# Attention and spectral mixing on one core: complex mode weights read in 16 KB rows, two modes on the two halves of the partitions

## The chip, the cores and the metric

The kernel runs on one core of a Trainium2 chip. The metric is the device time of one execution, in microseconds (us), as the median of three runs. The inputs and the output are float32. A trace of one execution, taken by the hardware profiler, goes with the times.

## The reference, cut to what matters

Two stages follow each other. The first is attention over a sliding window of 128 keys with a distance bias, on q, k, v of shape (8 batches, 8 heads, 576 tokens, 64). Its result is laid out as x of shape (8, 576, 512). The second stage mixes x in the frequency domain:

```python
X = np.fft.rfft(x, axis=1)                       # x: (8, 576, 512)
Xr, Xi = real(X[:, :64]), imag(X[:, :64])        # the 64 lowest modes
Yr = einsum('bmd,mde->bme', Xr, w_r) - einsum('bmd,mde->bme', Xi, w_i)
Yi = einsum('bmd,mde->bme', Xr, w_i) + einsum('bmd,mde->bme', Xi, w_r)
y = np.fft.irfft(Yr + 1j * Yi, n=576, axis=1)    # other modes are zero
u = x + y
out = u + np.maximum(u @ w_ch, 0.0)              # (8, 576, 512) float32
```

`w_r` and `w_i` are (64 modes, 512, 512) float32, 67 MB each. Every mode has its own complex matrix, and each is used once, for the 8 batches.

## The kernel before

**Attention.** The work is cut into 16 units: a batch and four of its heads. The list `STAGE` writes out by hand the order in which the steps of neighbouring units are issued: cast, transpose, evacuate, score, exp, mask, value, norm. Loads of q, k and v go out on SyncE's queue, two units ahead, each as soon as the raw tile that it fills has been cast. After a batch's second unit `spectrum` multiplies the batch's x by the table `F` of cosines and sines (TensorE, 20 matmuls, weights x of 128 channels taken every fourth, moving 128 columns of `F`), and `channels` copies the result from PSUM into `XC` (mostly on ScalarE), the stationary operand of the weight products. The spectrum's PSUM tile shares its buffer (`tp`) with the transposes of q and k.

**Weights.** A unit of weights is one matrix of one mode, 1 MB in HBM, cast to bfloat16 by the DMA that GpSimd issues: 128 partitions, each with four neighbouring rows of the matrix (8 KB read, 4 KB written). There are 127, since the imaginary matrix of mode 0 multiplies zeros. `load_w` loads single units: 14 into the pool `early`, 7 into the raw tiles that attention has finished with (`spare`), and 8 again into `early` (`again`). In attention a tiny copy by GpSimd (`gate`, L565) holds each load back until a cast of k is done. `load_packs` loads two units with one DMA (L491) into 6 and later 8 buffers, or one by one (L499) for the last four modes. The last unit comes in three parts.

**Products.** For a unit, four matmuls (L886) contract over 128 partitions each: `XC` gives 32 stationary columns (16 for the real, 16 for the imaginary output, 8 batches each), the weights are the 512 moving columns, and the result goes to 32 rows of the PSUM tile `acc`. The units of two modes go side by side on two column groups of the array. Four modes make a quad. `quad_end` scales it into bfloat16 (L608), transposes it (L612) and copies it to `YT`. From the ninth quad on, a list `side` gives TensorE one piece of other work at each step: `stream_spectra` (L631 to L637), `project` (L702, L711) and `augment` (L726 to L734), that is the inverse transform and the channel product of the first 32 modes. `warm` (L688) issues matmuls without use.

**The end.** For the last quad `late_end` and the code after the loop scale the late rows, transpose them, and patch the rows of the last modes into `Z` and `ZW` by small DMAs (`patch`, L648). Then 18 pieces of output are finished: a relu on ScalarE (L802), a sum on VectorE (L842), and a store on SyncE's queue.

Of the kernel before, what the change touches and what calls it, by code (L numbers as in the profile page):

```python
# [34 lines left out]
NC = 24  # L35

# [70 lines left out]
class _Attention:  # L107


    def __init__(self, tc, ctx, q, k, v, consts, x, XC, raw):  # L110
        self.tc, self.nc = tc, tc.nc
        self.q, self.k, self.v = q, k, v
        self.ident, self.F, self.FT = consts
# [256 lines left out]
    def spectrum(self, u, _):  # L370
        nc = self.nc
        b, g = self.units[u]
        if g < self.NG - 1:
            return
        NM = self.F.shape[2] // 2

        last = u == len(self.units) - 1
        xt = self.ps.tile([P, 2, 4, 2, NM], FP32, tag="tp")
        for a in range(4):
            for st in range(FULL + 1):  # L380
                nc.tensor.matmul(
                    xt[:, a // 2 if last else 0, a].rearrange("p r m -> p (r m)"),
                    lhsT=self.x[:, b, st, a::4],
                    rhs=self.F[:, st + (b % 2 if st == FULL else 0)].rearrange(
                        "p (m r) -> p r m", r=2),
                    start=(st == 0), stop=(st == FULL),
                )
        self.open["xt", u] = xt

    def channels(self, u, _):  # L390

        nc = self.nc
        b, g = self.units[u]
        if g < self.NG - 1:
            return
        xt = self.open.pop(("xt", u))
        NM = self.F.shape[2] // 2
        view = self.XC[:, : 4 * NC * NM].rearrange(
            "p (q s t b m) -> p q t s b m", q=2, s=3, t=2, b=8)[:, :, :, :, b]
        if u < len(self.units) - 1:  # L400
            src = xt[:, 0].rearrange("p (q t) r m -> p q t r m", q=2)
            nc.scalar.copy(view[:, :, :, 1:], src)
            nc.scalar.mul(view[:, :, :, 0], src[:, :, :, 1], -1.0)
        else:
            lo, hi = slice(0, 2), slice(2, 4)
            nc.scalar.copy(view[:, 0, :, 1:], xt[:, 0, lo])
            nc.scalar.mul(view[:, 0, :, 0], xt[:, 0, lo, 1, :], -1.0)
            nc.vector.tensor_copy(view[:, 1, :, 1:], xt[:, 1, hi])
            nc.vector.tensor_scalar_mul(view[:, 1, :, 0], xt[:, 1, hi, 1, :], -1.0)
# [3 lines left out]
def kernel(  # L413
# [21 lines left out]
    XC = const.tile([P, 4 * NC * NM + 16 * NM], BF16, name="XC")  # L435
    ident = const.tile([P, P], BF16, name="ident")
    F = const.tile([P, FULL + 2, 2 * NM], BF16, name="F")
    FT = const.tile([P, 2, S], BF16, name="FT")
    gate = const.tile([P, 8], BF16, name="gate")
# [14 lines left out]
    turns = []  # L454
    for g in range(NM // 4):
        for m in range(4 * g, 4 * g + 4, 2):
            turns += ([[2 * m, 2 * m + 2], [2 * m + 1, 2 * m + 3]] if g < LAST
                      else [[2 * m], [2 * m + 1], [2 * m + 2], [2 * m + 3]])
    spot = {i: k for k, i in enumerate(i for turn in turns for i in turn)}
    turns[1].remove(1)  # L460
    wq, homes, todo_w, again = {}, {}, [i for turn in turns for i in turn], []

    def load_w(n, pool, chosen=None):

        for i in ([i for i in todo_w if i not in again][:n] if chosen is None else chosen):
            todo_w.remove(i)
            src = (moe_w_r, moe_w_i)[i % 2][i // 2].rearrange("(p a) e -> p a e", a=4)
            homes[i] = pool
            t = spare.pop(0) if pool is None else pool.tile([P, 4, DM], BF16, tag="w", name="w")
            for part in ((slice(0, 4),) if i < 2 * NM - 1  # L470
                         else (slice(0, 2), slice(2, 3), slice(3, 4))):
                nc.gpsimd.dma_start(out=t[:, part], in_=src[:, part])
            wq[i] = [t[:, a] for a in range(4)]

    def load_packs(n, pool):

        for _ in range(n):
# [3 lines left out]
            assert len(pack) == 2  # L481
            t = pool.tile([P, 2, 4, DM], BF16, tag="w", name="w")
            kinds = {i % 2 for i in pack}
            for s, i in enumerate(pack):
                todo_w.remove(i)
                homes[i] = pool if s else False
                wq[i] = [t[:, s, a] for a in range(4)]
            m, w = pack[0] // 2, (moe_w_r, moe_w_i)
            if len(kinds) == 1:
                assert pack[1] == pack[0] + 2  # L490
                nc.gpsimd.dma_start(  # L491
                    out=t.rearrange("p s a e -> p s (a e)"),
                    in_=w[kinds.pop()][m : m + 2].rearrange("m (p a) e -> p m (a e)", a=4))
                continue
            for s, i in enumerate(pack):
                src = w[i % 2][i // 2].rearrange("(p a) e -> p a e", a=4)
                for part in ((slice(0, 4),) if i < 2 * NM - 1
                             else (slice(0, 2), slice(2, 3), slice(3, 4))):
                    nc.gpsimd.dma_start(out=t[:, s, part], in_=src[:, part])  # L499

    with ExitStack() as actx:
        at = _Attention(tc, actx, q, k, v, (ident, F, FT), x, XC, raw)
# [26 lines left out]
        nc.gpsimd.memset(XC[:, 4 * NC * NM :], 0.0)  # L529
# [40 lines left out]
    with ExitStack() as mctx:  # L570
# [13 lines left out]
        def late_end(acc):  # L584

            rows = slice(0, 96)
            yq = pool.tile([P, DM], BF16, tag="yq", bufs=3)
            nc.vector.tensor_scalar_mul(yq[rows], acc[rows], 2.0 / S)
            patch([(nc.gpsimd, b) for b in range(2, B)], yq, lambda b: Z[:, b // 2, 1], 0, 6)
            yield  # L590
            tr = lps.tile([P, 4, P], BF16, tag="tr", name="tr")
# [13 lines left out]
        def quad_end(acc, g):  # L605

            yq = pool.tile([P, DM], BF16, tag="yq", bufs=3)
            nc.vector.tensor_scalar_mul(yq, acc, 2.0 / S if g else norm)  # L608
# [4 lines left out]
            hf, mm = g // 8, 4 * (g % 8)  # L613
            for ri in range(2):
                src = tr.rearrange("p e (j c) -> p e c j", c=32)[:, :, 16 * ri : 16 * ri + B]
                dst = YT[:, hf, :, :, mm : mm + 4, ri]
# [240 lines left out]
        quads, side, recycle = [], [], list(again)  # L857
        ZW = Z = XW = FM = FC = pairs = wch = w2 = None
        K1 = spot[again[-1]]
        for g in range(NM // 4):  # L860
            if g == 0:
                lps.tile([P, 2, 4, P], BF16, tag="tr", name="tr")
            acc = (lps if g % 2 else ps).tile([P, DM], FP32, tag="acc", bufs=1, name="acc")
            if g == LAST:
                part_acc = ps.tile([P, DM], FP32, tag="pa", bufs=1, name="pa")
            for i in range(8):
# [13 lines left out]
                now = turns.pop(0) if turns and spot[turns[0][0]] == k else []  # L880
                for a in range(4):
                    for t in now:
                        m, ri = t // 2, t % 2
                        c0 = (a // 2 * 2 * NC + 16 * (1 - ri) + a % 2 * 8) * NM + m
                        into = part_acc if g == LAST and m < NM - 1 else acc
                        nc.tensor.matmul(  # L886
                            into[32 * (m % 4) : 32 * (m % 4) + 32],
                            lhsT=XC[:, c0 : c0 + 31 * NM + 1 : NM], rhs=wq[t][a],
                            start=(ri == 0 and a == 0), stop=(ri == (m > 0) and a == 3),
                            tile_position=(0, 32 * (m % 4)),  # L890
                        )
                own = next((t for t in homes if spot[t] == k), None)
                if own is None:
                    continue
                if recycle:
                    load_w(1, early, [recycle.pop(0)])
                elif homes[own] not in (early, None, False):
                    load_packs(1, homes[own])
# [33 lines left out]
                elif g > LAST - 2 and k < 2 * NM - 1 or g == LAST - 2 and not side:  # L932
                    warm()
                if g == LAST and i == 5:
                    quads.append(late_end(part_acc))
                    next(quads[0])
            if g < LAST:
                quads.append(quad_end(acc, g))
                next(quads[0])
# [5 lines left out]
            elif g == LAST - 1:  # L945
# [8 lines left out]
        zl = zps.tile([P, DM], FP32, tag="z0", name="zl")  # L954
        nc.tensor.matmul(zl, lhsT=ident, rhs=wch[:, 0], start=True, stop=True)
        sides = (slice(0, DM // 2), slice(DM // 2, DM))
        trs = (lps.tile([P, 4, P], BF16, tag="tr", name="tr"),
               zps.tile([P, 4, P], BF16, tag="z1", name="tr1"))
        for i, c in enumerate(sides):
            nc.scalar.mul(yq[96:, c], acc[96:, c], 2.0 / S)  # L960
            for et in (2 * i, 2 * i + 1):
                nc.tensor.transpose(trs[i][:, et, 96:], yq[96:, et * P : (et + 1) * P],
                                    ident[96:, 96:])
            nc.vector.tensor_copy(yT[:, 2 * i : 2 * i + 2, 96:],
                                  trs[i][:, 2 * i : 2 * i + 2, 96:])
        patch([(nc.sync, 0), (nc.gpsimd, 1)], yq, lambda b: Z[:, b // 2, 1])
        patch([(nc.gpsimd, b) for b in (2, 3, 4, 5, 6)], yq, lambda b: Z[:, b // 2, 1], 6)
# [4 lines left out]
        for i, c in enumerate(sides):  # L972
            zl = zps.tile([P, DM], FP32, tag=f"z{i}", name=f"zl{i}")
# [14 lines left out]
        patch([(nc.gpsimd, 7)], yq, lambda b: Z[:, b // 2, 1], 6)  # L988
# [40 lines left out]
```

## Time and profile before

| | |
|---|---|
| median of 3 runs | 437.81 us (437.63 to 439.78) |
| the profiled execution, its own time | 437.99 us |
| its span, first to last instruction | 436.1 us |
| TensorE, busy | 316.2 us (73%), 3488 matmuls |
| VectorE, busy | 184.5 us (42%) |
| ScalarE, busy | 162.3 us (37%) |
| GpSimd, busy | 90.2 us (21%) |
| read from HBM, written to it | 162.53 MB, 9.44 MB |
| mean granted TensorE clock | 0.862 |

Engines in the profile are PE (TensorE matmul), PEld (TensorE weight load), DVE (VectorE), ACT (ScalarE), POOL (GpSimd) and SP (SyncE); a "q" behind a name is the engine's queue of issues. L886 is line 886 of the kernel. GB/s in the profile counts the bytes written, so a weight that is read as float32 and written as bfloat16 counts half of what is read. The share of the DMA engines adds up the times of their packets, and packets of one DMA engine overlap a little, so it can be above 1. A matmul's own time in the profile includes its way through the array; how dense a run of them is shows in the distance from start to start.

### The profile page before, as it was taken

To read this page: it belongs to the slowest core of one execution; us is meant where nothing else is said; L and a number is where in the kernel's file an instruction comes from. 1 tells how busy PE (TensorE), PEld (TensorE's weight loads), DVE (VectorE), ACT (ScalarE), POOL (GpSimd) and SP (SyncE) were. 2 spreads that over 40 slices of the span, in tenths; PEclk is the share of its full clock that TensorE was granted. 3 is DMA by queue.
4 is the path that set the end of the run, shared out by engine and by line. 5 is a ranking of instruction groups with operands and counts; after the bars stand their busy time and mean duration, and the time that the engine had idled before them with its cause. 6 is when DMAs were issued, how large, how long until landed. Compare 5 with 4: busy or idle time off the path is not lost.

```text
span 436.1 us, 8292 instructions
## 1 busy us (share of the span) xinstructions
PE 316.2 (73%) x3488; PEld 177.7 (41%) x3509; DVE 184.5 (42%) x332; ACT 162.3 (37%) x211; POOL 90.2 (21%) x170
## 2 busy tenths in 40 slices
PE   5589899979686635543442487999889999788982
PEld 4367677757565312111111133444434444334430
DVE  7789799887783301000000021322213233122684
ACT  6949899988681000000000011322222322102780
POOL 8701010103424002222112110101111110012600
PEclk9969999999999955555555569999999999989997
DMA  8999999999999999999999999999999999998598
GB/s 285 326 311 310 290 316 300 307 298 299 252 217 212 215 215 213 214 214 214 215 212 214 214 215 214 215 214 215 215 214 214 215 215 215 213 215 153 190 378 311
DMA packets 50453, 105.54 MB, mean 242 GB/s; under 512 B 4032, under 2 KB 21072, under 8 KB 50416
## 3 DMA queue, kind: packets, MB, share of 16 engines
q0 software_dynamic: 19440, 68.41, 77.9%
q1 hardware_dynamic: 30976, 36.60, 25.3%
q8 instruction: 27, 0.44, 0.4%
q14 instruction: 10, 0.08, 0.1%
HBM read 162.53 MB, written 9.44 MB: 394 GB/s over the span
## 4 chain that ended last, share of the span: by engine, by line
DMA 71%; PE 10%; DVE 8%; issue 5%; POOL 2%; ACT 1%; SPq 1%; DVEq 0%; POOLq 0%; ACTq 0%
DMA w<-in_moe_w_i_dram 42%; DMA wch<-in_moe_w_ch_dram 8%; DMA qr<-in_q_dram 7%; DMA vr<-in_v_dram 6%; DVE o L842 3%; DMA qr<-in_moe_w_i_dram 3%; PE my L702 2%; DMA vr<-in_moe_w_r_dram 2%; DMA kr<-in_k_dram 2%; DVE vb L246 1%; PE acc L886 1%; PE av L344 1%; POOL Z L648 1%; PE my L659 1%; DVE att L318 1%
## 5 line engine op out<-in xcount | busy, mean ns | idle before, releaser
L886 PE MATMUL acc<-w,XC 128*32 128x512 bf16 x456 | 80.3, 478 | 68.5 <-DMA w<-in_moe_w_i_dram 34.2
L886 PEld LDWEIGHTS <-XC 128*32 128x32 bf16 x508 | 38.4, 147 | 109.2 <-issue 82.8
L307 ACT ACTIVATE att<-sc 128x1024 bf16<-128x1024 f32 x64 | 64.1, 1032 | 9.7 <-PE sc L297 9.6
L636 ACT CAST ZW<-zw 128x512 bf16<-128x512 f32 x8 | 4.7, 585 | 142.9 <-PE zw L634 142.9
L344 PE MATMUL av<-vb,att 128*128 128x132 bf16 (+1 forms) x576 | 38.4, 217 | 13.3 <-DVE x L360 8.6
L344 PEld LDWEIGHTS <-att 128*128 128x128 bf16 x704 | 36.6, 98 | 18.7 <-DVE x L360 12.0
L608 DVE TENSOR_SCALAR yq<-acc 128x512 bf16<-128x512 f32 x14 | 9.6, 687 | 81.8 <-PE acc L886 81.8
L702 PE MATMUL my<-wch,xT 128*64 128x512 bf16 x288 | 34.5, 381 | 5.7 <-ACT x L733 4.2
L711 ACT CAST XW<-my 128x512 bf16<-128x512 f32 x36 | 19.3, 589 | 50.5 <-PE my L659 50.5
L683 DVE COPY xT<-tr 128x1024 bf16<-128x1024 bf16 x18 | 12.4, 692 | 54.9 <-PE tr L681 54.9
L269 ACT COPY qkT<-tp 128x1152 bf16<-128x1152 bf16 x30 | 33.5, 1116 | 4.1 <-PE tp L263 3.6
L491 POOL DMA_DIRECT2D w<-in_moe_w_r_dram x22 | 15.6, 710 | 72.1 <-PE acc L886 46.1
L491 POOL DMA_DIRECT2D w<-in_moe_w_i_dram x23 | 16.3, 709 | 64.1 <-PE acc L886 45.3
L297 PE MATMUL sc<-qkT 64*64 64x256 bf16 (+2 forms) x640 | 25.1, 263 | 4.8 <-ACT qkT L269 1.2
L360 DVE TENSOR_TENSOR x<-av,rec 128x640 bf16<-128x640 f32 x32 | 26.4, 825 | 1.1
L702 PEld LDWEIGHTS <-xT 128*64 128x64 bf16 x288 | 17.1, 109 | 21.5 <-issue 9.1
L246 DVE CAST vb<-vr 64x1024 bf16<-64x1024 f32 x32 | 22.6, 708 | 0.2
L733 ACT CAST x<-my 128x512 bf16<-128x512 f32 x18 | 10.5, 585 | 31.6 <-PE my L659 31.6
L297 PEld LDWEIGHTS <-qkT 64*64 64x64 bf16 x640 | 14.5, 109 | 19.1 <-issue 16.0
L734 DVE CAST x<-my 128x512 bf16<-128x512 f32 x18 | 12.4, 692 | 21.7 <-PE my L659 21.7
L842 DVE TENSOR_TENSOR o<-yy,r 128x1024 f32<-128x1024 f32 (+1 forms) x20 | 20.3, 1059 | 2.1 <-ACT r L802 1.9
L318 DVE TENSOR_TENSOR att<-att,mask 128x1024 bf16<-128x1024 bf16 x32 | 20.5, 682 | 0.0
(137 smaller groups left out, 424.7 us busy)
## 6 DMA issues: line engine op xcount, KB each, us to landing
w<-in_moe_w_i_dram POOLq DMA_DIRECT2D x23, 1024.0 KB, 36.2
w<-in_moe_w_r_dram POOLq DMA_DIRECT2D x22, 1024.0 KB, 35.6
qr<-in_q_dram SPq DMA_DIRECT2D x16, 576.0 KB, 7.9
kr<-in_k_dram SPq DMA_DIRECT2D x16, 576.0 KB, 7.9
w<-in_moe_w_r_dram POOLq DMA_DIRECT2D x16, 512.0 KB, 14.2
vr<-in_v_dram SPq DMA_DIRECT2D x56, 128.0 KB, 7.6
w<-in_moe_w_i_dram POOLq DMA_DIRECT2D x13, 512.0 KB, 24.0
out_dram<-o SPq DMA_DIRECT2D x13, 512.0 KB, 5.0
```

The lines of the kernel that those rows point to most:

```text
L246: nc.vector.tensor_copy(self.vb[u % 2][row, :, :, :, W * half : W * half + D], src[row, :2])
L269: (self.nc.vector.tensor_copy if u < 2 and w == "q" else self.nc.scalar.copy)(dst.rearrange("q h (p j) -> q h p j", j=TPP), tp.rearrange(" ...
L297: nc.tensor.matmul(sc[64 * half : 64 * half + 64, e, j * 256 + c0 : j * 256 + c0 + n], lhsT=qkT[row, 1, h, k0 + j : k0 + P : 2], rhs=qkT[r ...
L307: self.nc.scalar.activation(self.att[u % 2][:, kt * 8 * P : (kt + 1) * 8 * P], sc.rearrange("p e n -> p (e n)"), AF.Exp, scale=1.0 / math. ...
L318: nc.vector.tensor_tensor(out=rows, in0=rows, in1=self.table[:, heads], op=ALU.mult)
L344: nc.tensor.matmul(bank[:, qt * W : qt * W + rhs[j].shape[1]], lhsT=att[:, o : o + P], rhs=rhs[j], start=(n == 0 and j == 0), stop=(n == l ...
L360: nc.vector.tensor_tensor(out=self.x[:, b, :, cs].rearrange("p t (h d) -> p h t d", h=2), in0=tiles[:, :, :, :D], in1=rec.unsqueeze(-1).br ...
L491: nc.gpsimd.dma_start(out=t.rearrange("p s a e -> p s (a e)"), in_=w[kinds.pop()][m : m + 2].rearrange("m (p a) e -> p m (a e)", a=4))
L702: nc.tensor.matmul(mm[ROWS[half]], lhsT=lhsT, rhs=wch[:, dt], start=(dt == 0), stop=False, skip_group_check=True,)
L711: nc.scalar.copy(XW[:, j, n], mms[n])
L842: nc.vector.tensor_tensor(out=o[:, c], in0=yy[:, c], in1=r[:, c], op=ALU.add)
L886: nc.tensor.matmul(into[32 * (m % 4) : 32 * (m % 4) + 32], lhsT=XC[:, c0 : c0 + 31 * NM + 1 : NM], rhs=wq[t][a], start=(ri == 0 and a == 0 ...
```

## The change

A pack is now one kind of matrix (real or imaginary) of two neighbouring modes: the even mode on partitions 0 to 63, the odd one on 64 to 127, eight neighbouring rows of a matrix to a partition. In HBM a pack is one stretch of 2 MB, and each partition's row is 16 KB read and 8 KB written. `load_packs` loads a pack with one DMA; only the last pack comes in four parts. `load_w` loads half a pack (four of the eight rows of each partition, 8 KB read). The order of packs is real, real, imaginary, imaginary for each two pairs of modes (`seq`).

The spectra follow that layout. A second table `F2` holds the modes sorted by even and odd (33 columns each for real and imaginary, `XM`), copied from `F` by GpSimd at the start. `spectrum` makes 80 matmuls for a batch in place of 20, with 64 stationary columns (every eighth channel), 66 moving ones, alternately on the two column halves of the array. `XC` has the even modes' channels on partitions 0 to 63 and the odd modes' on 64 to 127.

A product now contracts over 64 partitions, so a pack has 16 matmuls. Even modes go to one PSUM tile and odd ones to another, and two packs are interleaved so that four neighbouring matmuls sit on four different tiles of the array (two row halves, two column groups). Products are issued when four steps have gathered (two packs), or one pack in the last quad; buffers are given back then. Two PSUM tiles hold eight modes, and `quad_end` runs twice after every second quad. In the last quad modes 60 and 61 are finished early and 62 and 63 late (before: 60 to 62 early).

```diff
+XM = 33
...
-        for a in range(4):
+        xt = self.ps.tile([P, 8, P], FP32, tag="tp")
+        for a in range(8):
             for st in range(FULL + 1):
...
+                for par in range(2):
+                    nc.tensor.matmul(
+                        xt[64 * par : 64 * par + 64, a, : 2 * XM],
+                        lhsT=self.x[:, b, st, (a + 4 * par) % 8 :: 8],
+                        rhs=self.F2[:, st + (b % 2 if st == FULL else 0), par].rearrange(
+                            "p r m -> p (r m)"),
+                        start=(st == 0), stop=(st == FULL), tile_position=(0, 64 * par),
+                    )
...
+    def pack_rows(p):
+
+        w, m = (moe_w_r, moe_w_i)[p % 2], p // 2 * 2
+        return w[m : m + 2].rearrange("m (p a) e -> (m p) a e", a=8)
...
+            nc.gpsimd.dma_start(out=t, in_=rows[:, 4 * (i % 2) : 4 * (i % 2) + 4])
...
-                nc.gpsimd.dma_start(
-                    out=t.rearrange("p s a e -> p s (a e)"),
-                    in_=w[kinds.pop()][m : m + 2].rearrange("m (p a) e -> p m (a e)", a=4))
...
+            for part in ((slice(0, 8),) if p < PACKS - 1
+                         else (slice(0, 4), slice(4, 6), slice(6, 7), slice(7, 8))):
+                nc.gpsimd.dma_start(out=t[:, part].rearrange("p a e -> p (a e)"),
+                                    in_=rows[:, part].rearrange("p a e -> p (a e)"))
...
+    def products(packs, accs, quadrants):
...
+                todo.append([(ri, par, where, 64 * par, slice(64 * par, 64 * par + 64), a, wq[p][a],
+                              (a + 4 * par) % 8, mp, a == 7 and ri == (2 * mp + par > 0))
+                             for a in range(8) for par in range(2)])
+        if len({len(t) for t in todo}) == 1:
+            todo = [[m for i in range(0, 16, 2) for t in todo for m in t[i : i + 2]]]
+        for ri, par, where, row, rows, a, w, at_a, m, stop in (m for t in todo for m in t):
+            c0 = (at_a // 2 * 2 * NC + 16 * (1 - ri) + at_a % 2 * 8) * XM + m
+            o = 32 * where[par]
+            nc.tensor.matmul(
+                accs[par][o : o + 32], lhsT=XC[rows, c0 : c0 + 31 * XM + 1 : XM], rhs=w[rows],
+                start=(ri == 0 and a == 0), stop=stop, tile_position=(row, o),
+            )
...
+        modes = F.rearrange("p a (m w r) -> p a w r m", w=2, r=2)
+        for par in range(2):
+            nc.gpsimd.tensor_copy(F2[:, :, par, :, : XM - 1], modes[:, :, par])
+            nc.gpsimd.tensor_copy(F2[:, :, par, :, XM - 1 :], modes[:, :, 1, :, :1])
...
+                waiting.append(k)
+                done = []
+                if k % (2 if g == LAST else 4) == (1 if g == LAST else 3):
+                    products([seq[t // 2] for t in waiting[::2]], accs,
+                             (lambda mp: (mp % 4, mp % 4)) if g < LAST - 1
+                             else (lambda mp: (2 * (mp % 2), 2 * (mp % 2) + 1)))
+                    done = [t for t in waiting if t in homes]
+                    waiting.clear()
+                for own in done:
+                    if recycle:
+                        load_w(1, early, [recycle.pop(0)])
+                    elif homes[own] not in (early, None):
+                        load_packs(1, homes[own])
...
-        for i, c in enumerate(sides):
-            nc.scalar.mul(yq[96:, c], acc[96:, c], 2.0 / S)
+        for c in sides:
+            nc.scalar.mul(yq[96:, c], accs[1][96:, c], 2.0 / S)
+            nc.vector.tensor_scalar_mul(yq[64:96, c], accs[0][64:96, c], 2.0 / S)
```

## The prediction, as it was written before the result was known

> **What bounds the kernel now.** I read the page first, for where the DMA engines stand against the other engines.
>
> ```profile
> DMA  8999999999999999999999999999999999998598
> GB/s 285 326 311 310 290 316 300 307 298 299 252 217 212 215 215 213 214 214 214 215 212 214 214 215 214 215 214 215 215 214 214 215 215 215 213 215 153 190 378 311
> q0 software_dynamic: 19440, 68.41, 77.9%
> q1 hardware_dynamic: 30976, 36.60, 25.3%
> w<-in_moe_w_i_dram POOLq DMA_DIRECT2D x23, 1024.0 KB, 36.2
> ```
>
> All 16 DMA engines are at 90% or more from the second slice to the 36th. From slice 12 on the rate is flat at about 214 GB/s written, 428 read: weights alone. A pack of weights waits 36 us from issue to landing, so the queue is never short. The busy time by stages (us; engines, clock, DMA share, GB/s) says whether another engine is close behind.
>
> ```profile
> core 0: us, PE busy (x) PEld busy (x) DVE busy (x) ACT busy (x) POOL busy (x), PEclk, DMA share, GB/s
> 56.00:70.00 14.00, 12.82 (x239) 10.06 (x240) 13.27 (x25) 13.28 (x16) 1.99 (x6) 1.00 1.07 302
> 84.00:98.00 14.00, 10.91 (x208) 8.69 (x204) 11.36 (x20) 12.08 (x13) 1.23 (x3) 1.00 1.09 305
> 150.00:245.00 95.00, 39.76 (x168) 14.65 (x167) 5.90 (x24) 0.00 (x0) 18.42 (x31) 0.51 1.07 214
> 295.00:372.00 77.00, 69.36 (x592) 32.48 (x588) 20.52 (x35) 20.99 (x38) 10.45 (x17) 1.00 1.06 214
> ```
>
> Attention (to about 140 us) has three engines near 90% with the DMA engines full as well. At 150 to 245 us everything but the DMA is idle half the time. At 295 to 372 us PE is 90% busy, and the DMA rate doesn't move. The chain of waits (start, us, what) shows who sets the end there, and what follows the last weights.
>
> ```profile
> 333.71 1.10 PE acc L886 x8
> 334.81 0.29 issue
> 335.10 37.73 DMA w<-in_moe_w_i_dram
> 372.82 0.28 issue
> 373.11 24.25 DMA w<-in_moe_w_i_dram
> 397.41 1.04 PE pa L886 x4
> 398.47 0.70 DVE yq L588
> ```
>
> So the end is set by the weight stream, which lands its last part at about 402.4 us, and by 34 us of tail after it. The change is worth what it does to the rate of the stream, to any pause of it, and to the tail. For the price of a matmul the timeline (start, us, engine) has these runs:
>
> ```profile
> 37.07 0.63 PE L297 MATMUL sc<-qkT 64*64 64x256 bf16 x16
> 39.03 1.35 PE L381 MATMUL xt<-F,x 128*128 128x128 bf16 x20
> 44.74 0.96 PE L193 MATMUL ps<-ident,F 128*32 128x128 bf16 x32
> 333.71 1.08 PE L886 MATMUL acc<-w,XC 128*32 128x512 bf16 x8 [0.24 <-DMA w<-in_moe_w_i_dram]
> 405.15 0.39 PE L659 MATMUL mm<-ZW,FT 64*64 64x512 bf16 x4
> ```
>
> **The rows of 16 KB.** A pack is 1.05 MB written; at 214.4 GB/s that is 4.89 us, or 16 rows of 4 KB on each DMA engine, 305.6 ns a row. What can shrink is the part of a row that doesn't grow with its bytes. The trace's packets give it: rows of 4 KB show 324 ns and the few of 2 KB (parts of the last unit) 173 ns. So 151 ns belong to 2 KB and 22 ns are left; 324 - 305.6 = 18 of them lie beside the neighbouring packet, and 4 count. The page gives an upper end: q0's packets take 0.779 x 16 x 436.1 us / 19440 = 280 ns for 3519 B written (about 7040 read), q1's 57 ns for 1181 B; two such equations leave 12 ns a packet. The lower end is nothing, if a row is cut into pieces of 8 KB anyway; a loss is the fourth rival. I take 4 ns, from the same queue's own rows. Of 127 units 29 go by load_w with rows as before; 98 make 49 packs, 48 in whole rows. Each engine moves 8 rows fewer a pack: 8 x 4 ns x 48 = **-1.5 us** (0 to -4.6). The bytes stay.
>
> **The spectra.** Before, 20 matmuls (L381): 1.35 us, 59 ns from start to start, with 0.22 us for the last. Now 80, each with its own load of 64 columns and 66 moving columns. The loads price them, since matmuls on different columns overlap (L193's follow each other faster than 128 columns pass). L193 loads 32 columns of all 128 rows for each matmul and goes at 24 ns on average (its starts lie 13 to 15 ns apart where the queue is full), so 64 columns should take 26 to 30. I take 30, half the L381 distance: 80 x 30 ns + 0.2 = 2.6 us, +1.25 us a batch (from 24 ns: +0.8; from a full 59 ns: +3.6). What hides it is the DMA. ScalarE's copies of the spectrum (L402) start at 40.4, 56.0, 69.4, 83.4, 98.9, 114.5 us: a batch takes 13.5 us where ScalarE has no gap (69.4 - 56.0) and 15.5 where q waits for its DMA. A batch's loads (3.54 MB of q, k, v and about two units, 1.05 MB written) take 15.1 us at the 302 to 305 GB/s of these windows. So 1.6 us a batch is covered, and 1.25 just fits: **+0.2 us** for the place near 115 us where the queue is thin (0 to +1). Without cover it would be 8 x 1.25 = 10 us.
>
> The Trainium skill has a rule against this edit. "TensorEngine Tiling (Array Packing)", section "Restrictions", says that column tiling disables the fast weight load, and "TensorE: Matmul & The Clock Gate", section on LDWEIGHTS, puts a load at columns / 1.2 ns, so 53 ns for 64 columns. By it the 80 would take 4.4 us and the sum would be that of the third rival; L193's 13 to 15 ns for 32 columns speak against it (the formula gives 27), though its columns lie side by side and these are 16 bytes apart.
>
> **The products.** Before, 8 matmuls in two column groups: four rounds of about 215 ns and the last one's way out, 1.08 us a pack. Now 16 a pack, four at a time: L659 shows four tiles of 64 rows with 512 columns in 0.39 us, as long as one alone. Two packs are 8 rounds, about 1.95 us, against 2.16. PE has room and the DMA leads: 0. If they went two at a time, 3.7 us for two packs (9.8 us of stream) would put PE at 105% from 295 to 372 us, 4 us late at its end. The queue of 36 us and the idle of PE behind it take that: 0 too.
>
> **Refills and evacuations.** Buffers are given back for two packs at once, so a pack is asked for up to 4.9 us later, 31 us ahead in place of 36: 0. POOL has fewer issues (0.71 us for a pack as before, the last four modes no longer one by one). Two evacuations of 0.69 us (L608) in a row hold PE before the transposes as one did before; the next products come three steps later: 0. GpSimd's four copies for F2 (about 2 us by its copies L169, 1.04 us, less a smaller memset of XC, 0.96) stand ahead of the loads that it gates; POOL is idle from 20 to 25 us and its next load goes out at 26.2: 0, and +2 if that cover were gone, once.
>
> **The tail.** The last pack runs two at a time, 8 rounds; its last part (128 KB, as before) has two matmuls in one round, but the one before may still be on: +0.15 us. Then ScalarE took 0.65 us for 32 rows; now VectorE also scales 32 rows in two halves, by L408 (128x256 from PSUM) 0.43 each, ahead of its copies and of the patches: +0.3. Sum **+0.45** (0 to +1). Patches are as many as before.
>
> **Sum.** 437.99 (the profiled execution: span 436.1 and 1.9 around it) - 1.5 + 0.2 + 0.45 = 437.1. The median is 0.18 below the profiled one: 436.9 us.
>
> **The rivals.** (1) The fixed part of a row is larger, 12 ns: -4.6 us in place of -1.5, 433.8. For it: the page's two queues. Against it: a packet's time includes what overlaps (share 1.06). (2) The DMA cuts the rows and nothing is gained: 438.4. For it: no weight row of over 4 KB is written in this trace. (3) Slower: the strided loads of the spectra take as long as L381's whole distance or nearly, 48 (L193's 24 doubled) to 59 ns. A batch of compute is then 13.5 + 2.7 to 3.6 = 16.2 to 17.1 us against 15.1 of DMA, and the stream pauses for the difference, about six times: +7 to +12, 444 to 449. It decides from +1.6 us a batch on, that is 34 ns a matmul; place: PE before L402. ScalarE's wait for xt, 6.0 us in six, shows that nothing else stands between. (4) Slower: HBM gives stretches of 16 KB at doubled distances more slowly, and the packs' 48 x 4.89 = 235 us lose 1.5% in place of the gain: 438.4 + 3.5 = 441.9. For it speaks only that this pattern isn't in the trace.
>
> **How the numbers follow.** Forecast 0.40, (1) 0.20, (2) 0.14, (3) 0.17, (4) 0.09. A measurement of this kernel can tell about 0.5%, 2.2 us, from no change: 435.6 to 440.0. Below lie most of (1) and the low end of the forecast (a fixed part of 8 ns): 0.21. Above lie (3), most of (4): 0.25. Between: 0.54. The likeliest case alone spans 435.4 to 438.3. The range goes into (1) and over (4) to the edge of (3), 434.2 to 443, leaving out some 0.2.
>
> **What would show it.** Right: q0 with some 6000 packets fewer, the weight stage at 215 to 216 GB/s, the DMA row at 9 through attention, xt runs of 2.4 to 2.8 us, L402 starts at most 15.5 us apart, products x32 in about 2 us, the last part landing near 401. Wrong: a rate still at 214 (rival 2) or under 212 (4), DMA slices of 8 in attention with xt runs over 3.2 us (3), or the chain with PE in place of DMA after 295 us.

## The result and the profile after

The changed kernel takes 461.95 us in the median (458.31 to 464.70), the kernel before 438.38 in the same job: a ratio of 1.0528, with a 95% interval of 1.0469 to 1.0586. The profiled execution takes 462.55 us, its span is 460.8. The last weights land at 424.23 us (before: 402.37) and what follows them lasts 36.55 us (before: 33.71). So 21.9 of the 24.7 us of span are lost ahead of the last weights, and 2.8 behind them.

The same rows of the page as before:

```profile
PEclk9889899889799777955776557999999999989997
DMA  8999988998789999999999999999999999996498
GB/s 283 324 325 302 260 236 237 254 265 225 214 191 198 188 193 215 213 214 216 216 215 211 217 217 216 216 216 216 216 213 215 215 215 215 215 215 122 154 376 304
q0 software_dynamic: 13264, 68.41, 73.0%
q1 hardware_dynamic: 30976, 36.60, 23.8%
q8 instruction: 35, 0.57, 0.5%
w<-in_moe_w_i_dram POOLq DMA_DIRECT2D x24, 1024.0 KB, 28.8
```

The queue of the weights has 6176 packets fewer for the same 68.41 MB, and from slice 16 on the rate is mostly 215 to 217 in place of 214: the new rows do what they say. But slices 5 to 10 have fallen from about 300 to 225-265 GB/s, and 12 to 15 lie under 200. That is attention, and it is longer. The windows (us; engines, clock, DMA share, GB/s) show who is busy there:

```profile
core 0: us, PE busy (x) PEld busy (x) DVE busy (x) ACT busy (x) POOL busy (x), PEclk, DMA share, GB/s
56.00:70.00 14.00, 13.69 (x247) 11.84 (x245) 8.74 (x16) 9.79 (x12) 0.74 (x2) 1.00 0.92 247
84.00:98.00 14.00, 13.43 (x244) 11.01 (x243) 11.39 (x21) 10.67 (x11) 1.41 (x4) 0.95 0.88 247
295.00:372.00 77.00, 68.45 (x716) 32.85 (x718) 22.07 (x37) 19.92 (x36) 8.43 (x16) 1.00 1.03 215
```

In attention PE has gone from 78-92% to 96-98% and the DMA share from 1.07-1.09 to about 0.9: PE leads now. At 295 to 372 us PE's busy time and the rate are almost as before. The chain of waits (start, us, what) names the work:

```profile
91.51 1.20 DVE att L320 x2
92.87 0.83 DVE x L362
93.75 1.23 PE av L346 x20
94.98 4.95 PE xt L381 x78
99.93 0.97 PE sc L286 x2
```

The spectra stand in the chain with 5 us in six of the eight batches; before, they stand there in one, with 1.2 us. The timeline of PE in one batch:

```profile
113.08 5.01 PE L381 MATMUL xt<-F,x 128*64 128x66 bf16 x80
118.02 1.03 PE L286 MATMUL sc<-bias,ident 128*128 128x512 bf16 x2
118.99 0.64 PE L299 MATMUL sc<-qkT 64*64 64x256 bf16 x12
319.96 1.95 PE L517 MATMUL acc<-w,XC 64*32 64x512 bf16 x32
```

A spectrum matmul costs 60 ns from start to start, not 30, in all eight batches. In the trace two of them start 6 or 7 ns apart (the two column halves), then none for 114 ns. And the two matmuls at 118 us take 1.03 us, where other kernels below show 0.59: the clock has fallen.

```profile
core 0: us, PE busy (x) PEld busy (x) DVE busy (x) ACT busy (x) POOL busy (x), PEclk, DMA share, GB/s
113.00:115.00 2.00, 2.00 (x37) 1.95 (x35) 1.94 (x5) 1.21 (x2) 0.32 (x2) 1.00 0.94 260
116.00:118.00 2.00, 2.00 (x36) 1.95 (x34) 1.14 (x2) 0.00 (x0) 0.00 (x0) 0.50 1.10 354
120.00:122.00 2.00, 2.00 (x21) 1.05 (x19) 0.00 (x0) 1.90 (x2) 0.00 (x0) 0.50 1.01 287
```

Some 3 us into the run the granted clock goes to half and stays there until 123 us. The spacing of the spectrum matmuls doesn't mind; what comes next does.

The copies into XC now start at 43.5, 64.2, 81.4, 100.0, 118.1, 137.3 and 155.5 us: 18.67 us a batch in place of 14.73. From 64.2 to 81.4 us the clock stays at 1.00, and that batch takes 17.2 us: the prediction's 13.5 of compute and 3.65 more of spectra (5.0 less 1.35). In each of the four behind it the clock is at half for a time (0.86 to 0.88 on average), and they take 18.2 to 19.2 us. The first distance, 20.7 us, is the longest of all; it is longer than the others in every version with 80 matmuls (18.0 to 19.2 in those below); why is open.

### The profile page after: what moved, and what is told of

Same layout as the page of the kernel before. It is cut to its first block, busy times and chain, and to the rows that moved or that the text cites. A ratio compares the mean times of both kernels' runs of the same rounds, so it can differ in the third digit from the quotient of the medians.

```text
span 460.8 us, 10277 instructions
## 1 busy us (share of the span) xinstructions
PE 359.0 (78%) x4487; PEld 217.8 (47%) x4487; DVE 187.6 (41%) x336; ACT 164.5 (36%) x213; POOL 83.1 (18%) x172
## 3 DMA queue, kind: packets, MB, share of 16 engines
q0 software_dynamic: 13264, 68.41, 73.0%
## 4 chain that ended last, share of the span: by engine, by line
DMA 36%; PE 24%; issue 21%; DVE 11%; POOL 3%; ACT 2%; SPq 1%; DVEq 0%; POOLq 0%; ACTq 0%
DMA w<-in_moe_w_r_dram 20%; DMA wch<-in_moe_w_ch_dram 8%; PE xt L381 6%; PE acc L517 5%; DMA vr<-in_v_dram 5%; PE av L346 4%; POOL w L496 2%; DVE vb L248 2%; PE sc L286 2%; DMA qr<-in_q_dram 2%; DVE x L362 2%; DVE o L878 2%; DVE att L320 2%; PE sc L299 2%; PE pa L517 2%
## 5 line engine op out<-in xcount | busy, mean ns | idle before, releaser
L517 PE MATMUL acc<-w,XC 64*32 64x512 bf16 x924 | 86.9, 467 | 48.1 <-DMA w<-in_moe_w_i_dram 28.1
L517 PEld LDWEIGHTS <-XC 64*32 64x32 bf16 (+1 forms) x1012 | 44.1, 139 | 89.6 <-issue 77.4
L346 PE MATMUL av<-vb,att 128*128 128x132 bf16 (+1 forms) x576 | 40.3, 223 | 7.2 <-DVE att L320 4.3
L346 PEld LDWEIGHTS <-att 128*128 128x128 bf16 x704 | 38.4, 101 | 12.8 <-DVE x L362 6.4
L381 PE MATMUL xt<-F,x 128*64 128x66 bf16 x640 | 40.0, 290 | 1.2 <-DVE x L362 1.2
L381 PEld LDWEIGHTS <-x 128*64 128x64 bf16 x640 | 39.0, 216 | 1.7 <-DVE x L362 1.3
L496 POOL DMA_DIRECT2D w<-in_moe_w_i_dram x28 | 14.9, 536 | 89.3 <-PE acc L517 64.7
L496 POOL DMA_DIRECT2D w<-in_moe_w_r_dram x24 | 12.8, 535 | 91.9 <-PE acc L517 68.7
L299 PE MATMUL sc<-qkT 64*64 64x256 bf16 (+2 forms) x640 | 27.1, 280 | 2.1 <-ACT qkT L271 1.2
L361 DVE RECIPROCAL rec<-av 128x10 f32<-128x10 f32 x32 | 6.9, 217 | 46.5 <-PE av L346 46.5
L286 PE MATMUL sc<-bias,ident 128*128 128x512 bf16 x64 | 24.1, 465 | 1.6 <-ACT att L309 1.6
## 6 DMA issues: line engine op xcount, KB each, us to landing
w<-in_moe_w_i_dram POOLq DMA_DIRECT2D x24, 1024.0 KB, 28.8
w<-in_moe_w_i_dram POOLq DMA_DIRECT2D x10, 512.0 KB, 14.8
```

The lines of the kernel that those rows point to most:

```text
L286: nc.tensor.matmul(sc[:, e], lhsT=self.ident, rhs=self.bias[:, hv].rearrange("p j n -> p (j n)"), start=True, stop=False, skip_group_check ...
L299: nc.tensor.matmul(sc[64 * half : 64 * half + 64, e, j * 256 + c0 : j * 256 + c0 + n], lhsT=qkT[row, 1, h, k0 + j : k0 + P : 2], rhs=qkT[r ...
L346: nc.tensor.matmul(bank[:, qt * W : qt * W + rhs[j].shape[1]], lhsT=att[:, o : o + P], rhs=rhs[j], start=(n == 0 and j == 0), stop=(n == l ...
L381: nc.tensor.matmul(xt[64 * par : 64 * par + 64, a, : 2 * XM], lhsT=self.x[:, b, st, (a + 4 * par) % 8 :: 8], rhs=self.F2[:, st + (b % 2 if ...
L496: nc.gpsimd.dma_start(out=t[:, part].rearrange("p a e -> p (a e)"), in_=rows[:, part].rearrange("p a e -> p (a e)"))
L517: nc.tensor.matmul(accs[par][o : o + 32], lhsT=XC[rows, c0 : c0 + 31 * XM + 1 : XM], rhs=w[rows], start=(ri == 0 and a == 0), stop=stop, t ...
```

## The experiments

The theory was: the loads of 64 columns that lie 16 bytes apart are the price. Rivals: the split into column halves is the price (the rule that the prediction quoted), or the time is lost elsewhere.

**The loads alone.**

> The mixing is left out; this kernel only issues runs of matmuls with 66 (or 128) moving columns, each with its own load of stationary columns, and a dense run between them. Theory 'strided' (loads whose columns lie 16 bytes apart are slow): alternate halves of 64 columns go at 26 to 30 ns from start to start when the columns lie side by side, at about 60 ns when they lie 16 bytes apart, and the granted clock falls in the long strided run and not in the long dense-column one. Rival 'tiled' (a load for a part of the array's columns is slow whatever its stride, as the Trainium skill's rule has it, 53 ns for 64 columns): about 55 to 60 ns for both, and 26 ns or more for 32 columns side by side.

The timeline of PE (start, us, count at the end). L42 is the dense run between the others; L47, L52, L57, L62 and L67 load 64 columns on the two halves in turn, at distances of 2, 4, 8, 16 and 32 bytes; L102 and L107 load 128 columns at 8 and 16; L111 64 columns at 16 on one half alone:

```profile
27.36 0.84 PE L47 MATMUL xt<-f,x 128*64 128x66 bf16 x40
34.27 0.86 PE L52 MATMUL xt<-f,x 128*64 128x66 bf16 x40
41.21 1.42 PE L57 MATMUL xt<-f,x 128*64 128x66 bf16 x40
42.79 5.99 PE L42 MATMUL wm<-f,x 128*128 128x512 bf16 x27 [0.16 <-issue]
48.71 4.93 PE L62 MATMUL xt<-f,x 128*64 128x66 bf16 x80
53.80 7.68 PE L42 MATMUL wm<-f,x 128*128 128x512 bf16 x27 [0.16 <-issue]
61.41 2.60 PE L67 MATMUL xt<-f,x 128*64 128x66 bf16 x40
113.65 1.51 PE L102 MATMUL xt<-f,x 128*128 128x66 bf16 x40
121.04 2.56 PE L107 MATMUL xt<-f,x 128*128 128x66 bf16 x40
129.58 4.97 PE L111 MATMUL xt<-f,x 128*64 128x66 bf16 x40
```

With the last matmul's way out (about 0.2 us) taken off, a load and its matmul cost 16 ns at 2 and 4 bytes, 30 at 8, 60 at 16 and no more at 32. The two halves load at the same time, so one half needs twice that: 119 ns for 64 columns at 16 bytes (L111). A load of 128 columns and its matmul need 59 ns at 16 bytes and 33 at 8 (L107, L102). The 66 moved columns alone take 29 ns (a dense matmul of 512 takes 5.99 / 27 = 222 ns, 0.43 a column), 14 or 15 a matmul on two halves. So the 16 and the 33 are upper bounds of the load; the 30, 60 and 119 are the loads themselves. At 2 and 4 bytes a split costs nothing that shows; at 8 bytes and more it costs a factor of about two (2 x 30 against 33, 2 x 60 against 59). Side by side the expectation was 26 to 30 ns, too much. After L62 the dense run takes 7.68 us in place of 5.99: the clock again. In longer runs behind these, 200 matmuls at 16 bytes (L126) bring it to 0.50, 400 side by side (L131) leave it at 1.00.

The Trainium skill has two rules for this. "TensorEngine Tiling (Array Packing)", section "Restrictions", lets column tiling lose the fast weight load: the 40 matmuls of L47 in 0.84 us speak against a price for it side by side, L111 against L107 for it at a distance. "SBUF — State Buffer", section on Door 1, says that memory is read in lines of 16 bytes and that a line must be hit twice for full speed: the step from 8 to 16 bytes and the flat cost behind it agree, but at 8 bytes (two hits) the half-wide loads had doubled already.

**Side by side.**

```diff
-    lhsT=self.x[:, b, st, (a + 4 * par) % 8 :: 8],
+    lhsT=self.x[:, b, st, 64 * ((a + 4 * par) % 8) : 64 * ((a + 4 * par) % 8) + 64],
```

> The changed kernel, but each spectrum matmul takes 64 channels that lie side by side in place of every eighth (other channels than the reference's). 'Strided': 80 matmuls in 2.3 to 2.6 us, the clock stays at 1.00 in attention, and the time is 437.9 - 1.4 (rows) + 2.9 (tail) + 0 to 1 = 439 to 441. 'Tiled': 80 matmuls still in 5.0 us and the time stays at 462. Rival 'elsewhere' (refills, F2 or the new order hold attention up): matmuls in 2.4 us, but the time stays above 450.

Measured: 441.95 us (439.58 to 444.20), ratio to before 1.0053 (1.0023 to 1.0082), a microsecond above what was expected. The same 80 matmuls on the same two halves, of other channels:

```profile
85.97 1.46 PE L381 MATMUL xt<-F,x 128*64 128x66 bf16 x80
87.35 0.39 PE L286 MATMUL sc<-bias,ident 128*128 128x512 bf16 x1
```

20 of the 24 us are gone with one subscript. The split and the number of matmuls alone are not the cause; the distance of the columns under the split is.

**Twenty matmuls.**

```diff
-        for a in range(8):
+        for a in range(4):
...
+                nc.tensor.matmul(
+                    xt[:, 2 * a : 2 * a + 2, : 2 * XM], lhsT=self.x[:, b, st, a::4],
+                    rhs=F2[...],  # 132 columns
```

> The changed kernel with the 20 spectrum matmuls of before (128 columns, every fourth channel, 132 moving columns; the rows of the result are not those that the products need). 'Strided' and 'tiled': 1.4 us a batch, and the time is 437.9 - 1.4 + 2.9 = 439.4, 438.5 to 441. 'Elsewhere': above 450.

The layout that the products want is given up here. Measured: 440.55 us (439.19 to 443.64), ratio 1.0030 (0.9992 to 1.0067); the runs take 1.33 us, but for one. With the spectra at their old price no gain from the rest of the change shows, where the prediction had about 1 us.

**The kernel before with eighty.**

> The kernel before with its 20 spectrum matmuls replaced by 80 of 64 columns, every eighth channel, 128 moving columns, alternately on two column halves (the result is not the spectrum in the right places). 'Strided' and 'tiled': 5.0 us a batch, the clock falls to half after each, and the time is 437.9 + 21.7 = 459.6, 456 to 463. 'Elsewhere': below 447.

Only `spectrum` is changed: 80 matmuls of 64 columns at every eighth channel on the two halves, moving 128 columns of `F` (the results then lie in another order than the products take them). Measured: 454.51 us, ratio 1.0333 (1.0265 to 1.0401). The expectation, 456 to 463, was too high: the run takes the same 5.02 us as in the changed kernel, yet the loss is 15 us and not 21. A batch takes 17.52 us, not 18.67. The one difference in the run is 128 moving columns in place of 66, and the clock stays at 1.00 in the first seven batches (0.68 in the eighth).

**Wide.** The changed kernel, with 128 columns moved as well.

```diff
-    xt[64 * par : 64 * par + 64, a, : 2 * XM], ... rhs=self.F2[:, st + ..., par]
+    xt[64 * par : 64 * par + 64, a], ... rhs=wide[:, w0 : w0 + P]
```

> The changed kernel with one thing more: each spectrum matmul moves 128 columns instead of 66 (the 62 behind the wanted ones are neighbouring columns of the table and are not read afterwards); loads, strides, order and everything else stay. Theory 'clock': of the 3.94 us by which a batch of the changed kernel is longer than before (18.67 against 14.73 us from one XC copy to the next), some 1.5 us come from the granted clock, which falls to 0.5 in the spectra because matmuls of 66 columns at one load in 62 ns leave the array mostly empty. In the before_eighty run, with 128 columns at the same 62 ns, the clock stayed at 1.00 and a batch took 17.52 us. So here the run of spectrum matmuls stays at 5.0 us, the clock stays at 1.00, a batch takes 17.2 to 17.6 us, and the time falls by 6 to 10 us, to 453-456, though the array does twice the work. Rival 'length': the clock falls because a run of matmuls behind slow loads lasts over 3 us, whatever they move; then nothing changes: 462 (460-464). Rival 'columns': moved columns and loads add up, a matmul takes 62 + 62 columns at 0.4 ns = 88 ns, the run 7 us, and the time rises by 12-16 us, to 474-478.

Measured: 456.74 us (456.47 to 457.66), ratio 1.0383 (1.0326 to 1.0439): 5.2 us less than the changed kernel, less than the 6 to 10 of the expectation but far from 462 and from 474. A batch takes 17.55 us, the run 5.01, and right behind it the same work is fast again, at a clock of 1.00 (0.66 in the eighth batch alone):

```profile
111.08 5.01 PE L383 MATMUL xt<-F,x 128*64 128x128 bf16 x80
116.02 0.39 PE L286 MATMUL sc<-bias,ident 128*128 128x512 bf16 x1
117.59 0.59 PE L286 MATMUL sc<-bias,ident 128*128 128x512 bf16 x2
```

Moving twice as many columns, half of them for nothing, makes the kernel faster. The loads set the spacing either way; the next run shows what the columns do for the clock.

**Widths.** Where the clock gives way.

> Measures the granted clock by itself; nothing of the reference is computed. Between dense runs (56 matmuls of 128x128 by 512) stand runs of 200 matmuls, each with its own load of 64 columns at every eighth channel, on the two column halves in turn, moving 66, 80, 96, 112 and 128 columns; then 200 with 128 columns loaded at every eighth channel and 66 moved; then 200 with 64 columns at every fourth channel on one half alone and 66 moved. Theory 'clock' (how much of the array is at work sets it): each of the first five runs takes 12.0 to 12.5 us, one load in 61 ns; at 66 columns the granted clock falls to 0.5 after 3 to 5 us, at 128 it stays at 1.00, and it changes over somewhere between; the sixth run, 128 wide and 66 moved at 64 ns, has the array as full as 64 wide and 128 moved and stays at 1.00 if the cells count, and falls to 0.5 if only the moving share of the time counts. Rival 'length': the clock falls in all of the first five alike.

The timeline and the windows (granted clock third from the end):

```profile
32.90 12.07 PE L47 MATMUL xt<-f,x 128*64 128x66 bf16 x200
59.34 12.08 PE L52 MATMUL xt<-f,x 128*64 128x80 bf16 x200
84.52 12.05 PE L57 MATMUL xt<-f,x 128*64 128x96 bf16 x200
132.87 12.06 PE L67 MATMUL xt<-f,x 128*64 128x128 bf16 x200
156.96 12.22 PE L71 MATMUL xt<-f,x 128*128 128x66 bf16 x200
181.20 12.44 PE L75 MATMUL xt<-f,x 128*64 128x66 bf16 x200
```

```profile
36.00:39.00 3.00, 3.00 (x56) 3.00 (x54) 0.00 (x0) 0.00 (x0) 0.50 0.00 0
62.00:65.00 3.00, 3.00 (x56) 3.00 (x54) 0.00 (x0) 0.00 (x0) 0.69 0.00 0
88.00:92.00 4.00, 4.00 (x72) 4.00 (x72) 0.00 (x0) 0.00 (x0) 1.00 0.00 0
185.00:189.00 4.00, 4.00 (x69) 4.00 (x68) 0.00 (x0) 0.00 (x0) 1.00 0.00 0
```

With 66 columns the clock halves after 3 us, with 80 a little later, with 96, 112 and 128 never, nor in L71 and L75. It isn't the number of cells at work: L75 uses one half of the array, as much of the whole as L47, and keeps its clock. What fits all of them is the share of the time in which columns move, counted on one half of the array. In L47 both halves move at once, 29 ns in each 120: 24%. L111 and L126 of the first run, where the clock fell too, are at 24% as well. 80 columns make 29%, 96 make 35%, L75 (29 ns in 62) and L71 make 46%. The step lies between 29% and 35%. The expectation took it that L71 would tell cells from time; it doesn't, since columns move there for nearly twice the share of L47. Rival "length" falls.

The Trainium skill, "TensorE: Matmul & The Clock Gate", Part 1, tells of a gate with two states that watches how busy TensorE is over windows of 3.4 us, and warns of idle gaps. The two levels agree, 1.00 and 0.50 in the windows above, and so do the 3 us; here the clock fell on an engine whose busy time has no gap (3.00 us in 3.00) and that was waiting for its own loads.

**Every fourth.** The price that the prediction took, put into the kernel.

```diff
-    lhsT=self.x[:, b, st, (a + 4 * par) % 8 :: 8],
+    lhsT=self.x[:, b, st, (a + 4 * par) % 8 : (a + 4 * par) % 8 + 253 : 4],
```

> The changed kernel with the spectra's 64 channels taken at every fourth column of x instead of every eighth (half of the channels are then used twice and half not at all; the instructions, their number, their sizes and their order stay). It is the price that the prediction took, some 30 ns a matmul, put into the kernel: theory 'strided' says from the run of loads alone (40 of them at 8 bytes of distance in 1.42 us, at 16 bytes 60 ns each) that a run of 80 takes 2.4 to 2.9 us, that this hides in the batch as the prediction said, 14.6 to 14.9 us from XC to XC, and that the time is that of the kernel with side-by-side channels, 440 to 443. Rival 'cover': the prediction's cover of 1.6 us a batch was wrong too, and 1.1 to 1.5 us more of matmuls a batch come out in the end: 449 to 453. Rival 'any stride': a stride costs the same whatever it is: 460 to 464.

Measured: 444.00 us (442.65 to 446.00), ratio 1.0094 (1.0057 to 1.0132), just above the expectation. The run takes what the prediction said, and the clock holds:

```profile
102.31 2.67 PE L381 MATMUL xt<-F,x 128*64 128x66 bf16 x80
```

So 8 x (2.67 - 1.46) = 9.7 us of matmuls cost 2.05 us. After the first, batches take 14.9 us, 13.62 (the shortest of side_by_side) + 1.2: PE just leads.

**Half rows.** `side_by_side` again, with each pack in two transfers (`slice(0, 4), slice(4, 8)` in place of `slice(0, 8)`).

> The kernel with side-by-side channels (the spectra use wrong channels, at the price of contiguous loads), and each pack of the weight stage fetched by two transfers of half a row instead of one of a whole row; no other edit. It isolates the one term of the prediction that was a gain, 8 rows fewer per engine and pack at 4 ns, 1.5 us in all. Theory 'rows': from landing to landing a pack takes 4.93 us again (4.904 with whole rows, in the profile of the changed kernel), the weights land 1.2 to 1.8 us later relative to the first pack, and the packets of a queue are back at some 324 ns for half the bytes. Rival 'none': the 0.03 us a pack between before and after came from something else (the accumulators' order, the second read of weights), and the packs stay at 4.90.

From landing to landing between 262 us and 22 us before the last one, a pack takes 4.959 us on average; 4.916 with whole rows in side_by_side, 4.906 in the changed kernel, 4.942 before. Such an average holds a few packs that take 0.2 to 1.7 us longer than the rest; the medians are 4.92, 4.85, 4.87 and 4.89. Its last weights land at 406.37 us in place of 404.37. Rival "none" falls. The edit also doubles the number of transfers, and each puts one packet of 4 bytes (22 ns) on every DMA engine, so some 22 of the 43 ns between the averages may not be the rows'. One execution took 443.33 us.

## Why the prediction was wrong

It said 436.9 us and 434.2 to 443.0; the third rival's mechanism came, and came larger. Step by step:

**The rows of 16 KB** were right in the pack: -1.5 us stood in the sum. By the medians (4.894 us before, 4.865 in the changed kernel) a pack takes 29 ns less, 1.4 us for 48; half_rows, less its 22 ns, gives 21. The packets, 13264, and the rate of 215 to 217 are as foretold. But only part of it reached the end. From the landing of the 29th unit to the last landing it is 243.77 us before and 243.63 in the changed kernel, 242.6 to 243.7 in its versions with whole rows. What is missing lies in packs longer than the median, a few of them by 1 us and more. Of the 22 packs over 5.1 us in the traces of the eight versions (w_ch's landing left out) 19 have a packet of 16 KB of queue q8 ("instruction", 0.9 to 1.0 us) begin within them, of the others one in four. The page counts 35 of q8's packets, before 27. That they are the cause was not tried.

**The spectra** failed at the price. The sum had 30 ns from L193, whose columns lie side by side, and from half of L381's distance. Neither row had both a part-wide load and 16 bytes between its columns. And neither was limited by its loads. L381's load of 128 columns at 8 bytes takes at most 33 ns (L102), against 59 from start to start; its 128 moved columns take 55, at 0.43 each. On four column groups in turn 128 moved columns make 14 ns a matmul, which is L193's 13 to 15. So both rows showed moved columns, and half or double of them said nothing about a load. The price was 60 ns, the top of the third rival's 48 to 59. By the prediction's own working it gives, with its cover, (17.2 - 15.1) x 6 = 13 us; wide is 14.8 us slower than side_by_side.

**The cover** was nearly right. Wide has 8 x (5.01 - 1.46) = 28.4 us more of matmuls than side_by_side and is 14.8 us slower: 1.7 us a batch were hidden, where 1.6 had been worked out. But it isn't all there at the prediction's own price: every_fourth lost 2 us (1.0 of 1.2 us a batch hidden), where the sum had 0.2.

**The clock** was missing. No term or rival had it, though its own window at 150 to 245 us shows 0.51 where PE is half idle. It costs about 5 us (wide against the changed kernel: 5.2 in the medians, 5.0 at the last landing in the traces), with some 2 us of doubt, since the changed kernel's executions spread from 458.3 to 464.7.

**The products** were right: 32 in 1.95 us. **The refills** cost nothing, as foretold: a pack waits 28.8 to 30.0 us (medians) from issue to landing, so the queue is still never short.

**The tail** was mis-sized: +2.8 us, not +0.45. The timeline of the changed kernel around the last landing at 424.23:

```profile
420.01 0.67 DVE L616 TENSOR_SCALAR yq<-pa 32x512 bf16<-32x512 f32 x1
420.71 0.68 DVE L616 TENSOR_SCALAR yq<-acc 32x512 bf16<-32x512 f32 x1
421.44 0.37 PE L517 MATMUL acc<-w,XC 64*32 64x512 bf16 x1 [0.33 <-DVE yq L616]
426.44 0.76 DVE L1000 TENSOR_SCALAR yq<-pa 32x256 bf16<-32x256 f32 x2 [2.56 <-PE acc L517]
427.00 0.55 PE L1004 MATMUL tr<-ident,yq 64*128 64x64 bf16 x4 [0.28 <-DVE yq L1000]
```

The second-last pack landed at 419.22, but its products waited for pieces of `stream_spectra` (L667, L670) ahead of them and for VectorE, which still read the same PSUM tiles (0.33 us), so those of the last pack began at 424.46, after its last part had landed, and ended 2.17 us behind it. Before, PE took each part as it landed and ended 0.42 us behind the last:

```profile
402.42 0.38 PE L886 MATMUL acc<-w,XC 128*32 128x512 bf16 x1 [0.17 <-DMA w<-in_moe_w_i_dram]
```

That makes 1.75 us. The prediction priced the last two matmuls and took it that PE would be waiting for them. In twenty and half_rows PE happened to be in time (ends at 0.66 and 0.47 us), and the tails were 35.3 and 35.2 us; in wide it ended at 2.56 and the tail was 36.7. From the products to the first sum of the output (L859, before L823) it takes 3.86 us, before 3.11. Of these 0.75 us some 0.16 stand behind the scaling on two engines and the transposes, where 0.3 had been priced. Most of the rest is a wait of PE for ScalarE's copy of `zl` (L632), which PE before did not wait for; the second `zl` now lies in another pool (`lps`):

```profile
429.21 0.41 PE L798 MATMUL mm<-XW,ident 64*64 64x512 bf16 x4 [0.46 <-ACT F L632]
```

The other 0.3 us lie behind that. This was read from traces, and not tried by an edit.

**What stays open.** The first 29 units of weights have landed later than before, by 2.2 us in side_by_side (160.8 in place of 158.6 us) and 1.5 in twenty (160.1), though the spectra cost hardly more there. Part of it may be what half a clock did in single batches (in twenty the spectra of one batch took 2.35 us in place of 1.33, at 0.54); no run isolates it.

Put together, beside 438.4 to 439.2 for the kernel before: twenty and side_by_side at 440.6 and 442.0 (the tail and the open 1.5 to 2.2 us, less what arrived of the rows' gain), every_fourth 444.0, wide 456.7, the changed kernel 462.0. No version that was run beats the kernel before.

## What to carry to other kernels

Look at the bytes between the columns of a stationary operand before splitting a load: on half the array 64 columns cost at most 16 ns a load side by side, 30 at 8 bytes and 60 at 16, with both halves in use. Price a load from a row with the same width and the same distance, in which the moved columns are not the limit, or say that there is none and let the bounds reach to the next rows on the slow side. Where loads set the pace, more moved columns cost no time and can help: at 35% of the time and more the clock held, at 29% it fell to half for what came after.

## What the hardware showed

Loads of 64 columns on the two column halves run at the same time (60 ns each in turn in L62, 119 on one half alone in L111), so a split cost nothing that shows side by side (L47) and a factor of two at 16 bytes (L62 against L107). The granted clock fell to 0.50, 3 to 5 us into the run, on a TensorE whose busy time has no gap, when columns moved in 29% of the time or less, and it came back 2 to 4 us after dense work had begun.
